# Turning rows and columns in the dense part by transposing DMA transfers, on a TensorE-bound two-layer kernel

## The chip, the cores and the metric

The kernel runs on one core of one Trainium2 chip. The metric is device time in microseconds (us) of one launch. The kernel before was timed in three runs: 1625.38, 1627.13 and 1629.6 us, median 1627.13 us. A profile of one execution shows what each engine did: PE is TensorE (PEld its weight loads), DVE is VectorE, ACT is ScalarE, POOL is GpSimd, SP is the engine whose queue issues most of the transfers.

## The reference

Four stages follow each other on x of 2048 rows by 512 columns, and each adds its result to x: attention A, dense B, attention A, dense B, with the same weights both times.

```python
def _A_ref(x, mem0, Wq, Wk, Wv, Wo, seg_len):          # 32 heads of 128, M = 8, seg_len = 32
    mem = mem0
    for s in range(n_seg):                              # 64 segments, one after the other
        h = jnp.concatenate([mem, xs], axis=1)          # 8 memory rows + 32 rows of x
        q, k, v = (einsum('btd,dhe->bhte', h, W) for W in (Wq, Wk, Wv))
        scores = where(mask, einsum('bhqe,bhke->bhqk', q, k) * scale, -1e9)
        o = einsum('bhqk,bhke->bhqe', _softmax(scores), v)
        o = einsum('bhte,hed->btd', o, Wo)
        mem = o[:, :M, :].copy()                        # the memory of the next segment
        outs.append(o[:, M:, :])
def _B_ref(x, w1, w2):                                  # 512 -> 1376 -> 512
    return einsum('bsf,fd->bsd', maximum(einsum('bsd,df->bsf', x, w1), 0), w2)
x = x + _A_ref(_layernorm(x), A_mem0, ...)
x = x + _B_ref(_layernorm(x), B_w1, B_w2)
x = x + _A_ref(_layernorm(x), A_mem0, ...)
x = x + _B_ref(_layernorm(x), B_w1, B_w2)
```

The memory makes the segments of a layer a strict sequence: segment s+1 cannot start before the output projection of segment s has ended.

## The kernel before, in words

All weights stay in SBUF, in bf16. The kernel runs 68 steps. In step k the first attention layer works on segment k and the second on segment k-4 (`DELTA = 4`), side by side in the same instructions: the columns of `HT` hold 40 rows of the one (8 of memory, 32 of x) and 40 of the other. Steps 0 to 3 have only the first layer, steps 64 to 67 only the second. Within a step the heads come in five units: queries and keys (`queries_keys`), scores and softmax (`scores`), values (`step_values`), attention times values (`attend`), and then the output projection (`project`), whose PSUM bank `st` gives the next memory (evicted to `HT`) and the layer's output columns (evicted to `OX`).

The dense part stands between. After every second step `finish_pair(j)` takes the 64 rows of two segments of the first layer and, side by side, the 64 rows of two segments of the second layer that are done. The steps of it are, with the lines of the profile:

1. `OX` holds the attention's output with columns on the partitions. Four matmuls against the identity turn it into the PSUM bank `y` of the pool `fill` (helper `across`, L665).
2. DVE adds `y` to the rows `x` (tile `xg`, L884).
3. `layernorm` on DVE and POOL (L706, L709, L712, L713) writes the normalised rows to `xr` (L716); four matmuls turn them into another `fill` bank, and ACT or DVE copies that to `xnM` (L919, L921).
4. `dense_layer`: 44 matmul groups on `xnM` with w1, ReLU to `hT` (L765, L767), 11 with w2, and additions (L800, L804) that give the rows of the second layer's input and of the output.
5. For the first layer's half, a second `layernorm`: again four matmuls turn `xr`, and a copy writes `xnB`, from which POOL fills the columns of `HT` (`prep_x`, L941) at the start of the step that needs them.

There are 34 calls of `finish_pair` (30 of them with both halves) and 32 second layernorms. The 16 layernorms of the first layer's groups of 128 rows, marked `halved=True`, use the same function with another layout of the result.

The program's order is not that of the source. Every piece is an `op` of a `Plan` with the engine that it may run on, a cost, what it reads and writes, and a lag to the next engine. `Plan.order()` places them one by one by a priority: for PE work `PERIOD * step + PLACE[...]`, for the rest a due time worked back from it less `AHEAD[...]`; both tables are long lists of numbers. The instructions are then issued in that order on every engine and on every queue. SP's queue carries, per step, two transfers of old values (`V<-vh`, L1018), four of new values (`V<-vw`, L1024), the loads of x, and the stores of the output (L905), each behind the one before it. PSUM has five banks for `work`, one for `st` and two for `fill`.

Of the kernel before, what the change touches and what calls it, by code (L numbers as in the profile page):

```python
# [21 lines left out]
PE, ACT, DVE, POOL, SP, QUEUE = range(6)  # L22
# [4 lines left out]
WHOLE, COL64, EITHER, SOFT = range(4)  # L27
# [3 lines left out]
RULE = (0.0676, 338.0438, 3554579.0286, 1242705613.0663)  # L31
PERIOD = 42.8582
PLACE = {
    ("attend.mmu0.0", 0): 608.991, ("attend.mmu0.0", 1): 157.899, ("attend.mmu0.0", 2): -380.976,
    ("attend.mmu0.0", 3): -849.744, ("attend.mmu0.0", 4): -420.014, ("attend.mmu0.0", 5): 379.888,
    ("attend.mmu0.0", 6): -935.369, ("attend.mmu1.0", 0): 724.653, ("attend.mmu1.0", 1): 735.673,
    ("attend.mmu1.0", 2): 83.429, ("attend.mmu1.0", 3): -335.179, ("attend.mmu1.0", 4): 3.094,
    ("attend.mmu1.0", 5): -935.256, ("attend.mmu1.0", 6): -23.81, ("attend.mmu2.0", 0): -313.198,
    ("attend.mmu2.0", 1): -1055.43, ("attend.mmu2.0", 2): 351.452, ("attend.mmu2.0", 3): -29.526,
    ("attend.mmu2.0", 4): -812.532, ("attend.mmu2.0", 5): 234.539, ("attend.mmu2.0", 6): -65.699,  # L40
    ("attend.mmu3.0", 0): 13.451, ("attend.mmu3.0", 1): 157.484, ("attend.mmu3.0", 2): 133.291,
    ("attend.mmu3.0", 3): -203.514, ("attend.mmu3.0", 4): 192.222, ("attend.mmu3.0", 5): -84.323,
    ("attend.mmu3.0", 6): -139.89, ("attend.mmu4.0", 0): -853.255, ("attend.mmu4.0", 1): -244.026,
    ("attend.mmu4.0", 2): -305.761, ("attend.mmu4.0", 3): -104.638, ("attend.mmu4.0", 4): -89.602,
    ("attend.mmu4.0", 5): -204.344, ("attend.mmu4.0", 6): 50.714, ("dense_layer.mm.0", 1): 822.894,
    ("dense_layer.mm.0", 3): 717.325, ("dense_layer.mm.0", 6): 792.485, ("dense_layer.mm.1", 1): -268.282,
    ("dense_layer.mm.1", 3): 157.778, ("dense_layer.mm.1", 6): -380.794, ("dense_layer.mm.2", 1): 376.492,
    ("dense_layer.mm.2", 3): 130.965, ("dense_layer.mm.2", 6): -212.381, ("dense_layer.mm.3", 1): -70.602,
    ("dense_layer.mm.3", 3): 419.403, ("dense_layer.mm.3", 6): -774.382, ("dense_layer.mm.4", 1): -244.79,
    ("dense_layer.mm.4", 3): 367.889, ("dense_layer.mm.4", 6): -182.649, ("dense_layer.mm.5", 1): 943.633,  # L50
    ("dense_layer.mm.5", 3): -26.387, ("dense_layer.mm.5", 6): 595.003, ("finish_pair.turn.0", 1): -125.119,
    ("finish_pair.turn.0", 3): -175.437, ("finish_pair.turn.0", 6): -732.778, ("g0", 2): -902.623,
    ("g1", 2): -345.827, ("g2", 2): 376.933, ("g3", 2): -860.996, ("g4", 2): 261.098, ("g5", 2): -902.521,
    ("g6", 2): 262.286, ("g7", 2): 447.122, ("late_values.mmv0.0", 0): 7.391, ("late_values.mmv1.0", 0): 723.22,
    ("late_values.mmv2.0", 0): -33.087, ("late_values.mmv3.0", 0): -918.158, ("late_values.mmv4.0", 0): 711.016,
    ("late_values.mmv5.0", 0): -29.506, ("late_values.mmv6.0", 0): -417.119, ("late_values.mmv7.0", 0): -388.807,
    ("layernorm.turn.0", 1): -11.687, ("layernorm.turn.0", 3): 291.45, ("layernorm.turn.0", 6): 74.607,
    ("layernorm.turn.1", 1): 932.83, ("layernorm.turn.1", 3): -23.815, ("layernorm.turnr.0", 0): 130.977,
    ("layernorm.turnr.1", 0): 22.148, ("prepare.turns.0", 2): 138.08, ("project.mm.0", 0): -28.38,
    ("project.mm.0", 1): -813.549, ("project.mm.0", 2): -352.721, ("project.mm.0", 3): 338.425,  # L60
    ("project.mm.0", 4): -85.099, ("project.mm.0", 5): 395.603, ("project.mm.0", 6): 258.346,
    ("project.mm.1", 0): 382.886, ("project.mm.1", 1): 332.847, ("project.mm.1", 2): -815.345,
    ("project.mm.1", 3): 420.621, ("project.mm.1", 4): -904.087, ("project.mm.1", 5): 539.837,
    ("project.mm.1", 6): 66.403, ("project.mm.2", 0): 332.311, ("project.mm.2", 1): -807.177,
    ("project.mm.2", 2): -643.677, ("project.mm.2", 3): 169.374, ("project.mm.2", 4): 38.108,
    ("project.mm.2", 5): 154.46, ("project.mm.2", 6): -123.487, ("project.mm.3", 0): -94.659,
    ("project.mm.3", 1): -2.385, ("project.mm.3", 2): -392.671, ("project.mm.3", 3): 755.857,
    ("project.mm.3", 4): 239.419, ("project.mm.3", 5): 449.254, ("project.mm.3", 6): 237.48,
    ("project.mm.4", 0): -28.331, ("project.mm.4", 1): -89.329, ("project.mm.4", 2): 233.897,
    ("project.mm.4", 3): -897.55, ("project.mm.4", 4): 4.166, ("project.mm.4", 5): -271.575,  # L70
    ("project.mm.4", 6): 68.861, ("queries_keys.mmu0.0", 0): -114.972, ("queries_keys.mmu0.0", 1): -803.223,
    ("queries_keys.mmu0.0", 2): 449.473, ("queries_keys.mmu0.0", 3): -814.936, ("queries_keys.mmu0.0", 4): 64.492,
    ("queries_keys.mmu0.0", 5): -247.66, ("queries_keys.mmu0.0", 6): -321.229, ("queries_keys.mmu0.1", 0): -246.448,
    ("queries_keys.mmu0.1", 1): -83.345, ("queries_keys.mmu0.1", 2): -93.12, ("queries_keys.mmu0.1", 3): -67.094,
    ("queries_keys.mmu0.1", 4): -882.377, ("queries_keys.mmu0.1", 5): -142.63, ("queries_keys.mmu0.1", 6): -836.169,
    ("queries_keys.mmu0.2", 0): -921.465, ("queries_keys.mmu0.2", 1): -331.089, ("queries_keys.mmu0.2", 2): -36.099,
    ("queries_keys.mmu0.2", 3): -153.588, ("queries_keys.mmu0.2", 4): 0.628, ("queries_keys.mmu0.2", 5): -845.834,
    ("queries_keys.mmu0.2", 6): -937.81, ("queries_keys.mmu0.3", 0): -75.904, ("queries_keys.mmu0.3", 1): -26.436,
    ("queries_keys.mmu0.3", 2): -78.722, ("queries_keys.mmu0.3", 3): -83.815, ("queries_keys.mmu0.3", 4): -874.602,
    ("queries_keys.mmu0.3", 5): -285.858, ("queries_keys.mmu0.3", 6): -288.873,  # L80
    ("queries_keys.mmu1.0", 0): -287.689, ("queries_keys.mmu1.0", 1): -807.17, ("queries_keys.mmu1.0", 2): 138.905,
    ("queries_keys.mmu1.0", 3): -775.344, ("queries_keys.mmu1.0", 4): 333.755, ("queries_keys.mmu1.0", 5): -69.094,
    ("queries_keys.mmu1.0", 6): -299.934, ("queries_keys.mmu1.1", 0): -894.335,
    ("queries_keys.mmu1.1", 1): -300.828, ("queries_keys.mmu1.1", 2): -195.096,
    ("queries_keys.mmu1.1", 3): -407.541, ("queries_keys.mmu1.1", 4): -99.416, ("queries_keys.mmu1.1", 5): -928.29,
    ("queries_keys.mmu1.1", 6): -1007.777, ("queries_keys.mmu1.2", 0): -397.855,
    ("queries_keys.mmu1.2", 1): -271.199, ("queries_keys.mmu1.2", 2): -95.574, ("queries_keys.mmu1.2", 3): -424.872,
    ("queries_keys.mmu1.2", 4): -828.244, ("queries_keys.mmu1.2", 5): -84.504, ("queries_keys.mmu1.2", 6): -365.113,
    ("queries_keys.mmu1.3", 0): -267.974, ("queries_keys.mmu1.3", 1): -319.862, ("queries_keys.mmu1.3", 2): 11.67,
    ("queries_keys.mmu1.3", 3): -410.531, ("queries_keys.mmu1.3", 4): 44.01, ("queries_keys.mmu1.3", 5): -391.768,  # L90
    ("queries_keys.mmu1.3", 6): -213.718, ("queries_keys.mmu2.0", 0): -65.556, ("queries_keys.mmu2.0", 1): -240.632,
    ("queries_keys.mmu2.0", 2): 64.693, ("queries_keys.mmu2.0", 3): 448.514, ("queries_keys.mmu2.0", 4): 417.76,
    ("queries_keys.mmu2.0", 5): 347.423, ("queries_keys.mmu2.0", 6): -104.214, ("queries_keys.mmu2.1", 0): -34.178,
    ("queries_keys.mmu2.1", 1): 23.812, ("queries_keys.mmu2.1", 2): -196.254, ("queries_keys.mmu2.1", 3): -337.37,
    ("queries_keys.mmu2.1", 4): 139.933, ("queries_keys.mmu2.1", 5): -92.169, ("queries_keys.mmu2.1", 6): 434.453,
    ("queries_keys.mmu2.2", 0): 129.446, ("queries_keys.mmu2.2", 1): 68.117, ("queries_keys.mmu2.2", 2): -78.718,
    ("queries_keys.mmu2.2", 3): -0.671, ("queries_keys.mmu2.2", 4): 460.034, ("queries_keys.mmu2.2", 5): 252.252,
# [103 lines left out]


def t_dve(n, rate=1):
    return 0.065 + 1.042e-3 * n / rate


PART, MASKED = {ACT: 0.13, DVE: 0.10}, {ACT: 0.11, DVE: 0.065}


def t_pool(n):  # L210
    return 0.06 + 2.2e-3 * n


# [1119 lines left out]
```

## Time and profile before

| | |
|---|---|
| median of 3 runs | 1627.13 us (1625.38 to 1629.6) |
| span of the profiled execution, first to last instruction | 1624.3 us |
| its own time | not listed with the page; the runs' median lies 2.8 us over the span |
| PE busy | 1584.0 us (98%), 43678 matmuls |
| PE weight loads | 1378.5 us (85%) |
| DVE, ACT, POOL busy | 1031.9 us (64%), 1095.1 us (67%), 139.2 us (9%) |
| granted TensorE clock | 0.998 |
| DMA, mean | 39 GB/s over the span |
| two steps in the middle (evictions of `st` to `HT` at 779.41 and 827.52 us) | 48.1 us |

The chain that ended last is followed back from the last instruction to whatever released each one: an engine's share of it is time that the end of the kernel depended on. Matmuls overlap in the pipeline, so the mean of one in the list of groups (200 ns) is a latency; what a matmul costs the stream is the distance to the next, and that is what the chain of a stretch shows.

### The profile page before, as it was taken

What the parts mean: (1) busy time and instruction counts of PE and PEld (TensorE: products, weight loads), DVE (VectorE), ACT (ScalarE), POOL (GpSimd) and SP (SyncE); (2) the same over time, 40 slices, a digit from 0 to 9 for tenths busy, and PEclk for the clock granted to TensorE, in tenths of its full rate; (3) what the DMA queues carried; (4) which work ended last, traced back from release to release, by engine and by line L of the source; (5) the groups of instructions that cost most, each with busy time, mean ns of one, the idle gap of its engine ahead of it and who ended that gap; (6) DMA issues with size and microseconds to landing.
All of it is one profiled execution on the core that took longest, in us unless ns stands there. A gap on an engine that the chain in (4) does not pass through costs nothing.

```text
span 1624.3 us, 95837 instructions
## 1 busy us (share of the span) xinstructions
PE 1584.0 (98%) x43678; PEld 1378.5 (85%) x43746; DVE 1031.9 (64%) x2930; ACT 1095.1 (67%) x2813; POOL 139.2 (9%) x362
## 2 busy tenths in 40 slices
PE   7999999999999999999999999999999999999997
PEld 4688888888888888888888888888888888888886
DVE  4466756666665675676566567566656756665665
ACT  5567767766676776766677676667667766766664
POOL 4210000000000000100000000000000000000000
PEclk9999999999999999999999999999999999999999
DMA  9711001111100110111011011101101000000000
GB/s 372 264 23 33 19 22 29 23 27 34 34 21 21 29 25 25 35 28 26 22 30 25 26 35 28 25 22 26 27 25 28 23 21 19 17 20 19 19 6 6
DMA packets 42885, 63.37 MB, mean 39 GB/s; under 512 B 15400, under 2 KB 28816, under 8 KB 42480
## 3 DMA queue, kind: packets, MB, share of 16 engines
q1 hardware_dynamic: 35984, 35.88, 8.8%
q0 software_dynamic: 5328, 20.32, 3.3%
q8 instruction: 342, 5.60, 1.4%
q10 hardware_dynamic: 1168, 1.06, 0.2%
q14 instruction: 63, 0.52, 0.1%
HBM read 33.50 MB, written 11.93 MB: 28 GB/s over the span
## 4 chain that ended last, share of the span: by engine, by line
PE 94%; DVE 3%; issue 1%; ACT 1%; POOL 0%; DMA 0%; DVEq 0%; POOLq 0%; ACTq 0%
PE work L665 39%; PE st L665 19%; PE fill L998 15%; PE fill L665 12%; PE work L1166 4%; PE work L1082 3%; DVE es L1093 0%; DMA hT<-in_A_x_dram 0%; DVE mx L1097 0%; ACT HT L919 0%; PE fill L789 0%; DVE sm L1107 0%; DVE vw L921 0%; DVE PT L1149 0%; DVE es L1100 0%
## 5 line engine op out<-in xcount | busy, mean ns | idle before, releaser
L665 PE MATMUL work<-HT,Wq_sb 128*128 128x80 bf16 (+2 forms) x10208 | 369.3, 200 | 8.2 <-ACT HT L919 8.1
L665 PE MATMUL work<-HT,Wk_sb 128*128 128x80 bf16 (+2 forms) x10144 | 368.2, 200 | 2.4 <-issue 1.5
L665 PEld LDWEIGHTS <-Wq_sb 128*128 128x128 bf16 (+1 forms) x10208 | 330.4, 103 | 25.8 <-ACT HT L919 11.6
L665 PEld LDWEIGHTS <-Wk_sb 128*128 128x128 bf16 (+1 forms) x10144 | 333.4, 103 | 17.9 <-issue 3.5
L665 PE MATMUL st<-OT,Wo_sb 128*128 128x80 bf16 (+1 forms) x8704 | 339.7, 199 | 3.0 <-ACT OT L919 1.3
L665 PEld LDWEIGHTS <-Wo_sb 128*128 128x128 bf16 x8704 | 319.8, 99 | 11.7 <-issue 4.1
L919 ACT CAST qT<-work 128x320 bf16<-128x320 f32 (+1 forms) x484 | 197.7, 408 | 119.1 <-PE work L665 83.7
L998 PE MATMUL fill<-Wv_sb,HT 128*64 128x512 bf16 x2176 | 272.7, 381 | 0.5 <-POOL HT L938 0.5
L919 ACT CAST kT<-work 128x320 bf16<-128x320 f32 (+1 forms) x539 | 220.1, 409 | 58.5 <-PE work L665 18.7
L1147 ACT ACTIVATE PT<-work,half 128x320 bf16<-128x320 f32 (+2 forms) x448 | 200.6, 467 | 31.5 <-PE work L665 15.0
L919 ACT CAST vw<-fill 128x512 bf16<-128x512 f32 x227 | 132.8, 585 | 105.1 <-PE fill L998 103.0
L919 ACT CAST OT<-work 128x320 bf16<-128x320 f32 (+1 forms) x394 | 151.9, 413 | 76.4 <-PE work L1166 76.3
L1093 DVE TENSOR_TENSOR es<-work,maskb 128x320 f32<-128x320 f32 (+2 forms) x340 | 133.2, 402 | 60.3 <-PE work L1082 48.9
L998 PEld LDWEIGHTS <-HT 128*64 128x64 bf16 x2176 | 106.9, 110 | 70.5 <-issue 0.8
L884 DVE TENSOR_TENSOR xg<-xg,fill 128x512 f32<-128x512 f32 (+1 forms) x34 | 23.4, 688 | 185.9 <-PE fill L665 185.9
L1104 ACT ACTIVATE es<-es 128x320 f32<-128x320 f32 (+2 forms) x340 | 134.8, 406 | 7.4 <-DVE es L1100 3.5
L1100 DVE TENSOR_TENSOR es<-es,mx 128x320 f32<-128x320 f32 (+2 forms) x340 | 133.7, 404 | 2.6
L1097 DVE TENSOR_REDUCE mx<-es 128x8 f32<-128x320 f32 (+2 forms) x340 | 132.1, 399 | 3.6
L1124 DVE TENSOR_TENSOR P<-es,sm 128x320 bf16<-128x320 f32 (+2 forms) x338 | 131.1, 405 | 4.4
L1107 DVE TENSOR_REDUCE sm<-es 128x8 f32<-128x320 f32 (+2 forms) x340 | 130.9, 395 | 1.2 <-ACT es L1104 1.1
L1149 DVE TENSOR_SCALAR PT<-work,half 128x320 bf16<-128x320 f32 (+2 forms) x232 | 103.2, 454 | 26.6 <-PE work L665 24.3
L800 DVE TENSOR_TENSOR xg<-xg,fill 64x512 f32<-64x512 f32 x30 | 20.4, 681 | 140.5 <-PE fill L665 140.5
(98 smaller groups left out, 1801.7 us busy)
## 6 DMA issues: line engine op xcount, KB each, us to landing
V<-vw SPq DMA_DIRECT2D x240, 48.0 KB
V<-vh SPq DMA_DIRECT2D x120, 64.0 KB
Wq_sb<-in_A_Wq_dram POOLq DMA_DIRECT2D x2, 2048.0 KB, 21.0
Wk_sb<-in_A_Wk_dram POOLq DMA_DIRECT2D x2, 2048.0 KB, 25.4
Wo_sb<-in_A_Wo_dram POOLq DMA_DIRECT2D x2, 2048.0 KB, 37.1
vh<-vg SPq DMA_DIRECT2D x32, 128.0 KB
Wv_sb<-in_A_Wv_dram POOLq DMA_DIRECT2D x1, 2048.0 KB, 11.4
vh<-w_sb POOLq DMA_DIRECT2D x4, 512.0 KB, 5.3
```

What stands on the lines that cost most here:

```text
L665: nc.tensor.matmul(out_[u:v, :], lhsT=lhsT[:, u:v], rhs=rhs, start=start, stop=stop, tile_position=(0, u), **more)
L919: nc.scalar.copy(out=out_, in_=in_)
L998: nc.tensor.matmul(vp[64 * b:64 * b + 64, :], lhsT=cols(c4), rhs=Wv_sb[:, c4, n * 512:(n + 1) * 512], start=(c4 == 0), stop=(c4 == NC4 - 1 ...
L1093: nc.vector.tensor_tensor(out=flat(es[:, A]), in0=flat(sp[:, A]), op=ALU.add, in1=maskb[:, a_lo:a_hi, :].unsqueeze(2).to_broadcast([128, n ...
L1097: nc.vector.tensor_reduce(out=mx[:, As], in_=es3(), axis=AX.X, op=ALU.max)
L1100: nc.vector.tensor_tensor(out=es3(), in0=es3(), op=ALU.subtract, in1=mx[:, As].unsqueeze(2).to_broadcast([128, ns * na, L]))
L1104: nc.scalar.activation(out=es[:, A], in_=es[:, A], func=ACTF.Exp, scale=SCALE)
L1107: nc.vector.tensor_reduce(out=sm[:, As], in_=es3(), axis=AX.X, op=ALU.add)
L1124: (nc.gpsimd if eng == POOL else nc.vector).tensor_tensor(out=o, in0=flat(es[:, A]), op=ALU.mult, in1=sm[:, As].rearrange("p (a s) -> p a ...
L1147: nc.scalar.activation(out=o, in_=i, func=ACTF.Copy, scale=half[:, b:b + 1])
L1149: nc.vector.tensor_scalar_mul(out=o, in0=i, scalar1=half[:, b:b + 1])
L1166: nc.tensor.matmul(o[u:u + cols, :, a, :], lhsT=V[:, p, e0 + u:e0 + u + cols], rhs=PT[:, a, 2 * i + h2, :, :], start=True, stop=True, tile ...
```

## The change

In the dense part, the three turns (of `OX`, and of `xr` in both layernorms) are no longer matmuls. Each is one `dma_start_transpose` issued by SP: `OX` goes to a tile `y` in SBUF (of the pool `xr`, which has one buffer), `xr` goes straight to `xnM` or `xnB`. The copies from PSUM to `xnM` and `xnB` fall away, and so does a `fill` bank for each turn. `OX` is turned whole, all 128 rows, also where only one half of them is used; so its two tiles are set to zero by POOL at the start. The 16 `halved` layernorms keep their matmuls. `RULE`, `PLACE`, `AHEAD` and `PAIRED` are other numbers throughout, so that the order of all work is another one.

```diff
-RULE = (0.0676, 338.0438, 3554579.0286, 1242705613.0663)
+RULE = (0.077, 191.201, 3554579.029, 1242705613.066)
 ...
+XBAR = 0.5, 0.2, 2.6
 ...
+        for i, t in enumerate(p_ox.tiles):
+            def zero_ox(t=t):
+                nc.gpsimd.memset(t[:], 0.0)
+
+            plan.op(POOL, 0.4, zero_ox, w=[("oxz", i)])
 ...
     def layernorm(x, rows, xnT, lo=0, n=128, to=None, halved=False):
-        ln, xn, tp = p_ln.buf(), p_xr.buf(), b_fill.buf()
+        ln, xn, tp = p_ln.buf(), p_xr.buf(), b_fill.buf() if halved else None
 ...
-            else:
-                copy_on(eng, xnT[:, :, to:to + n], i.rearrange("p (c t) -> p c t", c=NC4))
+        def turn_far():
+            nc.sync.dma_start_transpose(out=xnT[:, :, to:to + n], in_=xn[R, :])
 ...
         plan.op(DVE, 0.453 + pd, norm, r=[x, ln, *rows], w=[xn])
+        if not halved:
+            plan.op(SP, XBAR[0] + XBAR[1] * NC4 * n / 128, turn_far, r=[xn], w=[xnT], lag=XBAR[2])
+            return xnT
         plan.op(PE, 0.01 + 1.72e-3 * n, turn, r=[xn, "ident"], w=[tp], tile=EITHER, count=4)
 ...
     def finish_pair(j):
-        x, ox, y = x_tiles[j], ox_tiles[j], b_fill.buf()
+        x, ox, y = x_tiles[j], ox_tiles[j], p_xr.buf()
 ...
-        def turn(cols):
-            T = slice(0, 128 if 1 in act else PR)
-            for c4 in range(NC4):
-                across(cols, y[:, c4 * 128:(c4 + 1) * 128], ox[:, c4, T], ident[:])
+        def turn():
+            nc.sync.dma_start_transpose(out=y[:, :].rearrange("t (c d) -> t c d", c=NC4),
+                                        in_=ox[:, :, :].rearrange("p c t -> p (c t)"))
 ...
-        plan.op(PE, 0.23, turn, r=[ox, "ident"], w=[y], tile=EITHER, count=4)
+        plan.op(SP, XBAR[0] + XBAR[1] * NC4, turn, r=[ox], w=[y], lag=XBAR[2])
 ...
-            copy_op(NC4 * SEG * len(aa), rows, r=[wo, ("taken", k)], w=[ox])
+            copy_op(NC4 * SEG * len(aa), rows, r=[wo, ("taken", k), ("oxz", 0), ("oxz", 1)], w=[ox])
```

## The prediction, made before the run

> **What bounds the kernel now.** I began with the page: span, busy shares and the chain that ended last.
>
> ```profile
> span 1624.3 us, 95837 instructions
> PE 1584.0 (98%) x43678; PEld 1378.5 (85%) x43746; DVE 1031.9 (64%) x2930; ACT 1095.1 (67%) x2813; POOL 139.2 (9%) x362
> PE 94%; DVE 3%; issue 1%; ACT 1%; POOL 0%; DMA 0%; DVEq 0%; POOLq 0%; ACTq 0%
> PE work L665 39%; PE st L665 19%; PE fill L998 15%; PE fill L665 12%; PE work L1166 4%; PE work L1082 3%; DVE es L1093 0%; DMA hT<-in_A_x_dram 0%; DVE mx L1097 0%; ACT HT L919 0%; PE fill L789 0%; DVE sm L1107 0%; DVE vw L921 0%; DVE PT L1149 0%; DVE es L1100 0%
> ```
>
> PE carries 94% of the chain; the other engines have a third of the time to spare. The end depends on how much PE has to do, and on little else. The waits of PE's weight loads, for the 60 or so steps with both layers (158 to 1518 us), say how little:
>
> ```profile
> PEld L665 <- ACT HT L919: 11.3, 26, 0.4
> PEld L665 <- DVE P L1124: 6.7, 28, 0.3
> PEld L665 <- issue: 2.8, 9, 0.4
> ```
>
> These three are all: 20.8 us in 1360. PE waits about 0.35 us a step, mostly for the eviction of the new memory to `HT`. So a microsecond taken from PE there is a microsecond off the end, as long as nothing new makes it wait.
>
> What the turns cost PE I read from the chain of two steps in the middle (779.4 to 827.5 us), whose columns are start, length, work:
>
> ```profile
> 783.29 0.22 PE fill L665 x4
> ...
> 787.38 0.22 PE fill L665 x8
> ...
> 826.79 0.12 PE fill L665 x4
> ```
>
> By the timeline of the same stretch these are the turn of `OX` (783.12), of `xr` for `xnM` (787.20, in eight half-width matmuls) and of `xr` for `xnB` (826.63). A pair of steps spends 0.22 + 0.22 + 0.12 = 0.56 us on them. The same timeline shows what lies around them:
>
> ```profile
> 779.52 0.38 ACT L919 CAST OX<-st 128x256 bf16<-128x256 f32 x1
> ...
> 783.55 0.69 DVE L884 TENSOR_TENSOR xg<-xg,fill 128x512 f32<-128x512 f32 x1 [6.13 <-PE fill L665]
> ...
> 786.18 0.55 DVE L716 TENSOR_SCALAR xr<-xg,ln 128x512 bf16<-128x512 f32 x1 [1.00 <-POOL ln L713]
> ...
> 794.10 1.96 PE L665 MATMUL fill<-xnM,w_sb 128*64 128x128 bf16 x64
> ...
> 808.69 0.55 DVE L716 TENSOR_SCALAR xr<-xg,ln 64x512 bf16<-64x512 f32 x1 [0.99 <-POOL ln L713]
> ...
> 827.43 0.52 POOL L941 COPY HT<-xnB 128x128 bf16<-128x128 bf16 x2 [7.59 <-ACT xnB L919]
> ```
>
> `OX` is complete at 779.90, the addition begins at 783.55. `xr` is complete at 786.73 and first used by PE at 794.10, 7.4 us later. The second `xr` is complete at 809.24 and read by POOL at 827.43, 18 us later. There the dense part has time to give away. At the end of the kernel it has none:
>
> ```profile
> 1611.34 0.27 ACT L919 CAST OX<-st 128x128 bf16<-128x128 f32 x1 [0.64 <-PE st L665]
> ...
> 1612.10 0.69 DVE L884 TENSOR_TENSOR xg<-xg,fill 64x512 f32<-64x512 f32 x1 [2.06 <-PE fill L665]
> ...
> 1614.72 0.55 DVE L716 TENSOR_SCALAR xr<-xg,ln 64x512 bf16<-64x512 f32 x1 [0.99 <-POOL ln L713]
> ...
> 1616.16 2.61 PE L665 MATMUL fill<-xnM,w_sb 128*128 128x64 bf16 x44 [0.46 <-ACT xnM L919]
> ...
> 1621.05 0.47 SPq L905 DMA_DIRECT2D out_dram<-ob  x1
> ```
>
> Every row waits for the one above it: the last pair's dense part runs alone.
>
> **What a transfer takes.** No transposing transfer is in this trace, so I bound it by plain ones. The shortest that can be followed on SP's queue is a load of 128 KB in the ramp, issued at 111.70 and awaited by DVE until 113.81, so 2.1 us. The last store (SP, out of SBUF, 64 KB) is issued at 1621.05 and the span ends at 1624.3: 3.2 us at most. Of POOL's issues a 128 KB store took longest, the last of the rows here:
>
> ```profile
> 111.70 0.35 SPq L825 DMA_DIRECT2D xe<-in_A_x_dram  x1
> 113.81 0.69 DVE L706 BATCH_NORM_STATS2 ln<-xe 128x6 f32<-128x512 bf16 x1 [2.38 <-DMA xe<-in_A_x_dram]
> xh<-OX POOLq DMA_DIRECT2D x1, 128.0 KB, 7.1
> ```
>
> So 2.1 to 7.1 us. I take 4.0 us from the source being ready to the result being usable: nearest is the store of 3.2 us, same queue and same source, and a turn moves up to twice its bytes and must be handed from DVE or ACT to SP and back. (The planner books 1.3 us on SP's queue and 2.6 more, the diff's `XBAR`; that is an input of its order and no measurement, and the sum doesn't use it.)
>
> **The change, part by part.**
>
> Removed from PE: 30 full pairs x 0.56 = 16.8 us; pairs 0 and 1 have a half-width `xr` in both layernorms, 0.22 + 0.12 + 0.12 = 0.46 each, 0.9; pair 32 has no second layernorm, 0.34. Sum 18.0 us. The last pair is counted in the tail.
>
> Removed from ACT and DVE: 34 copies to `xnM` (0.69 us on DVE, 0.59 on ACT) and 32 to `xnB` (0.37), some 34 us in all, on engines busy to two thirds. I count nothing: their lateness shows only in PE's 20.8 us, and of that the `HT` wait is a latency, not a load. Two `fill` banks are shared by fewer users; PE waited for no `fill` bank in that list, so nothing again.
>
> Tail: `OX` ready 1611.61 to addition 1612.10 is 0.49 us, becomes 4.0, +3.5. `xr` ready 1615.27 to first matmul 1616.16 is 0.89, becomes 4.0, +3.1. Sum +6.6 us; with 2.1 us it is +2.8, with 7.1 +12.8. [...]
>
> Middle: with 4.0 us, `y` lands at 783.9 (addition 0.4 us later than now), `xnM` at 791.1, before 794.10, and `xnB` at 813.2, before 827.43. At 7.1 us `xnM` would be 3.3 us late and the later 18 us would take that up. Cost 0, unless the order places users too early.
>
> SP's queue: three issues more per pair. Plain issues take 0.36 (`V<-vh`) and 0.72 us (`V<-vw`, median of 120); even 1.5 us each is 4.5 in 48, and the queue mostly waits. What stands behind a turn that waits for `OX` or `xr` are the value transfers, and behind those `attend` on PE. At 783 to 788 and 809 to 813 us the queue was empty, so I count 0; above, it could make `attend` late.
>
> Start: POOL sets two tiles to zero. Its nearest rows are 0.20 us (a memset of a quarter of the tile) and 0.61 (a cast of 64x512), so 0.4 to 1.2 us, on the path only if it stands before a weight load's issue. I take 0, since POOL is free before `OX` is needed at 54 us.
>
> Ramp: pair 0 has its second `xr` at 97.7 and step 4 starts at 111; three turns longer by about 3 us each still fit. Cost 0.
>
> New order: bounded from both sides by PE's waits. A perfect one could win all 20.8 us, one that doubles them would lose 20.8. I take 0, for the same rules and the same limits made it.
>
> Sum: -18.0 + 6.6 = -11.4 us. The profiled span becomes 1612.9; the page lists no time of its own for that execution, and the median of the runs lies 2.8 us over its span, so the forecast is 1615.7 us.
>
> **The rivals.**
>
> *Slow turns.* Each takes 7.1 us, as the slowest 128 KB transfer here. The middle hides it, the tail pays 12.8: -5.2, so 1621.9 us. For it: both are 128 KB and nothing here has shown a transposing one. Against: that row fell in the busiest stretch of DMA (over 260 GB/s).
>
> *The order loses (slower than before).* At the change of step PE waits 0.4 us for `HT`, in 26 of the 57 steps; in the others the last two w2 matmuls (804.84 us, 0.60 us of PE) stand in that gap. The turns were small pieces that could stand anywhere, and the dense work now comes up to 4 us later. If pieces no longer meet the gaps, each of 60 steps loses more. It decides from 11.4 / 60 = 0.19 us a step. If the 0.35 us doubles, it is +20.8: -11.4 + 20.8 = +9.4, so 1636.5 us. For it: every number of the order is new and PE has 1.5% of slack. Against: the rest of PE's work, and so what can fill gaps, is the same.
>
> *Half-way.* The gaps take 0.15 to 0.25 us a step: 1625 to 1630 us, no change.
>
> *Not what it says.* The 16 `halved` layernorms keep PE; 64 of their turns stay, and I've not counted them. So this changes nothing.
>
> **How the numbers follow.** The measurement can tell 0.3% (4.9 us) from no change. Forecast (turns of 2.1 to 5 us, order as good: 1609 to 1619) 0.46; slow turns 0.14, both faster; half-way 0.11; the order loses 0.29. So faster 0.60, same 0.11, slower 0.29. The range goes from 1608 (turns at 2.1 us give 1611.9, an order 4 us better) to 1638, just over the doubled waits: about 5% lie below and 13% above. The forecast's own range is 1609 to 1619.
>
> **What would show it right or wrong.** After the change no `fill<-ident,OX` is left, and `fill<-ident,xr` only for `halved` groups; PE has some 400 to 600 matmuls fewer. The 57 steps between the evictions to `HT` at 158.8 and 1518.5 us take 47.7 us a pair now and would take 47.1. The tail from the last `OX` eviction to the end, 13.0 us now, becomes about 19.6. PE's waits from 158 to 1518 us stay near 21 us. Wrong would be: more than 32 us of waits for `HT`, `P` or `V` there, or waits of PE for `xnM`.

## The result and the profile after

The change took 1620.24 us (median of 4 runs, 1619.77 to 1621.06) against 1627.35 us before (4 runs, 1625.38 to 1629.6): ratio 0.9953, 95% interval 0.9939 to 0.9967. That is 7.1 us faster; 11.4 were forecast (1615.7 us). The profiled execution took 1621.06 us over a span of 1619.3, the slowest of its four.

The page after: span, busy times, then the chain that ended last by engine and by line.

```profile
span 1619.3 us, 94084 instructions
PE 1573.6 (97%) x42673; PEld 1355.0 (84%) x42673; DVE 1050.2 (65%) x2974; ACT 1058.4 (65%) x2672; POOL 160.7 (10%) x395
PE 95%; ACT 2%; DMA 1%; POOL 1%; issue 1%; DVE 1%; POOLq 0%; SPq 0%; DVEq 0%; ACTq 0%
PE work L671 40%; PE st L671 19%; PE fill L1006 16%; PE fill L671 11%; PE work L1174 4%; PE work L1090 3%; ACT OT L927 1%; DMA xr<-OX 0%; ACT HT L927 0%; PE fill L798 0%; DMA xnM<-xr 0%; DMA V<-vw 0%; ACT es L1112 0%; POOL ln L719 0%; ACT qT L927 0%
```

PE is still the bound (95% of the chain) with 1005 matmuls fewer on record. New in the list of lines is `ACT OT L927` with 1%: the eviction before the output projection.

To see where the time went I cut the span at evictions of `st` to `HT`: that of step 5 (158.8 us before, 161.5 after), that of step 62, and that of step 66, the last. "Middle" is the 57 steps that the prediction named.

| us | start to step 5 | middle | step 62 to 66 | last to end | span |
|---|---|---|---|---|---|
| before | 158.8 | 1359.7 | 76.5 | 29.3 | 1624.3 |
| after | 161.5 | 1346.2 | 77.7 | 33.9 | 1619.3 |
| difference | +2.7 | -13.5 | +1.2 | +4.6 | -5.0 |

The medians differ by 7.1 and the two profiled spans by 5.0: each profile is one execution. That of after is 0.8 us over its median. A run's time lies some 1.8 us over its span here (1621.06 and 1619.3), so the profiled one of before is, by estimate, 1.3 us under its median.

**The middle.** By the medians an even step took 25.32 us and takes 24.85; an odd one took 22.13 and takes 22.23. The two turns of the even step (0.44 us of PE) came back in full, the one of the odd step (0.12) did not. The chain shows why. Start, length and work at the end of an odd step, before:

```profile
1205.53 0.43 PE work L1166 x12
1205.96 0.07 PE work L665 x2
1206.03 0.12 PE fill L665 x4
...
1206.18 1.31 PE st L665 x32
```

and at the same place after:

```profile
1151.37 0.16 PE work L1174 x4
...
1151.55 0.43 ACT OT L927
...
1152.03 1.31 PE st L671 x32
```

The four `fill` matmuls (0.12 us) and some others filled the time until `OT` was evicted and the last part of the projection could run. Without them PE stands still for ACT instead. The waits of PE's weight loads from 158 to 1518 us (total, times, longest) say the same:

```profile
PEld L671 <- issue: 17.0, 49, 0.4
PEld L671 <- ACT HT L927: 12.0, 29, 0.4
PEld L671 <- DVE P L1132: 9.6, 26, 0.4
```

38.6 us, and 39.1 with one more row, against 20.8 before. The wait for `HT` stayed; "issue" rose by 14. Of its 17.0 us, 5.1 stand before loads of `Wo_sb`, each of which starts within 0.01 us of a matmul that waited for `OT`. The other 11.9 stand before loads of `Wq_sb`, at one place of the new order, where the chain has no gap. One of them, and the chain there:

```profile
1140.47 1.19 PEld L671 LDWEIGHTS <-Wq_sb 128*128 128x128 bf16 x32 [0.41 <-issue]
...
1139.67 0.86 PE fill L1006 x8
1140.54 3.14 PE work L671 x84
```

So most of the rise costs the stream nothing: the matmuls of the whole stretch waited 4.0 us for `OT` (1.3 before) and 7.9 for `HT`, as before.

**A turn.** All turns of `OX` and all to `xnM`, in the view by tile: ns on SP's queue (min, median, max), first and last start.

```profile
L888 SPq DMA_TRANSPOSE xr<-OX x34: 1190/1237/2829, 78.0 to 1602.1; - x34
L736 SPq DMA_TRANSPOSE xnM<-xr x34: 1171/1215/2024, 86.8 to 1607.8; - x34
```

SP is held for 1.24 us. The tail, by the timeline, shows the whole turn:

```profile
1601.81 0.27 ACT L927 CAST OX<-st 128x128 bf16<-128x128 f32 x1 [1.05 <-PE st L671]
1602.10 1.19 SPq L888 DMA_TRANSPOSE xr<-OX  x1
1604.54 0.69 DVE L892 TENSOR_TENSOR xg<-xg,xr 64x512 f32<-64x512 f32 x1 [3.60 <-DMA xr<-OX]
...
1607.16 0.55 DVE L722 TENSOR_SCALAR xr<-xg,ln 64x512 bf16<-64x512 f32 x1 [0.99 <-POOL ln L719]
1607.77 1.17 SPq L736 DMA_TRANSPOSE xnM<-xr  x1
1610.12 2.61 PE L671 MATMUL fill<-xnM,w_sb 128*128 128x64 bf16 x44 [8.35 <-DMA xnM<-xr]
...
1612.66 2.56 PE L798 MATMUL fill<-w_sb,hT 128*64 128x256 bf16 x22
```

`OX` is ready at 1602.08 and added from 1604.54: 2.46 us (0.49 before). `xr` is ready at 1607.71 and used from 1610.12: 2.41 us (0.89 before). Together +3.5 us. The matmuls with w2 took 2.56 us where they had taken 1.42, +1.1. That is the clock (0.52, before 0.96); the last but two figures of a row are the granted clock, the DMA share follows. After, w1 and w2:

```profile
1610.10:1612.60 2.50, 2.48 (x44) 2.48 (x43) 0.00 (x0) 0.77 (x2) 0.00 (x0) 0.50 0.02 7
1612.60:1615.30 2.70, 2.62 (x24) 1.78 (x22) 0.26 (x2) 0.28 (x1) 0.00 (x0) 0.52 0.00 0
```

and w2 before:

```profile
1618.70:1620.20 1.50, 1.42 (x23) 1.15 (x22) 0.25 (x2) 0.28 (x1) 0.00 (x0) 0.96 0.00 0
```

w1 ran at half clock in both (0.50; before from 1616.10 to 1618.70 us). In the trace's record of the clock the low stretch lasts 3.4 us before (1615.39 to 1618.81) and 10.2 after (1604.96 to 1615.20). PE had stood idle for 3.3 us before the turn of `xr` at 1615.33, and with the change it does so for 8.4 us before w1. What sets the length of the low stretch is not shown.

### The profile page after: what moved, and what is told of

Its sections match the earlier page's. It is cut to its first block, busy times and chain, and to the rows that moved or that the text cites. A ratio compares the mean times of both kernels' runs of the same rounds, so it can differ in the third digit from the quotient of the medians.

```text
span 1619.3 us, 94084 instructions
## 1 busy us (share of the span) xinstructions
PE 1573.6 (97%) x42673; PEld 1355.0 (84%) x42673; DVE 1050.2 (65%) x2974; ACT 1058.4 (65%) x2672; POOL 160.7 (10%) x395
## 3 DMA queue, kind: packets, MB, share of 16 engines
q10 hardware_dynamic: 1168, 1.06, 0.2%
## 4 chain that ended last, share of the span: by engine, by line
PE 95%; ACT 2%; DMA 1%; POOL 1%; issue 1%; DVE 1%; POOLq 0%; SPq 0%; DVEq 0%; ACTq 0%
PE work L671 40%; PE st L671 19%; PE fill L1006 16%; PE fill L671 11%; PE work L1174 4%; PE work L1090 3%; ACT OT L927 1%; DMA xr<-OX 0%; ACT HT L927 0%; PE fill L798 0%; DMA xnM<-xr 0%; DMA V<-vw 0%; ACT es L1112 0%; POOL ln L719 0%; ACT qT L927 0%
## 5 line engine op out<-in xcount | busy, mean ns | idle before, releaser
L671 PE MATMUL work<-HT,Wk_sb 128*128 128x80 bf16 (+2 forms) x9184 | 357.3, 199 | 11.5 <-ACT HT L927 9.3
L671 PE MATMUL work<-HT,Wq_sb 128*128 128x80 bf16 (+2 forms) x10624 | 357.6, 200 | 0.0
L1006 PE MATMUL fill<-Wv_sb,HT 128*64 128x512 bf16 x2176 | 281.8, 383 | 0.9 <-POOL HT L946 0.5
L927 ACT CAST kT<-work 128x320 bf16<-128x320 f32 (+1 forms) x517 | 211.8, 410 | 107.5 <-PE work L671 66.3
L927 ACT CAST qT<-work 128x320 bf16<-128x320 f32 (+1 forms) x505 | 207.7, 412 | 73.7 <-PE work L671 25.7
L927 ACT CAST OT<-work 128x320 bf16<-128x320 f32 (+1 forms) x351 | 132.6, 414 | 129.2 <-PE work L1174 128.6
L1155 ACT ACTIVATE PT<-work,half 128x320 bf16<-128x320 f32 (+1 forms) x406 | 181.8, 477 | 8.7 <-DVE PT L1157 4.0
L927 ACT CAST vw<-fill 128x512 bf16<-128x512 f32 x228 | 133.9, 587 | 76.3 <-PE fill L1006 73.4
L1157 DVE TENSOR_SCALAR PT<-work,half 128x160 bf16<-128x160 f32 (+2 forms) x274 | 116.2, 445 | 31.4 <-PE work L671 29.7
L892 DVE TENSOR_TENSOR xg<-xg,xr 128x512 f32<-128x512 f32 (+1 forms) x34 | 23.5, 692 | 161.1 <-DMA xr<-OX 160.9
L1090 PEld LDWEIGHTS <-qT 128*40 128x40 bf16 x4096 | 87.4, 98 | 34.6 <-ACT qT L927 0.3
```

The source lines that it names most:

```text
L671: nc.tensor.matmul(out_[u:v, :], lhsT=lhsT[:, u:v], rhs=rhs, start=start, stop=stop, tile_position=(0, u), **more)
L927: nc.scalar.copy(out=out_, in_=in_)
L1006: nc.tensor.matmul(vp[64 * b:64 * b + 64, :], lhsT=cols(c4), rhs=Wv_sb[:, c4, n * 512:(n + 1) * 512], start=(c4 == 0), stop=(c4 == NC4 - 1 ...
L1090: nc.tensor.matmul(v[64 * g2:64 * g2 + L, a, i, b, :], lhsT=qT[:, hi, a * L:(a + 1) * L], rhs=kT[:, hi, a * L:(a + 1) * L], start=True, st ...
L1155: nc.scalar.activation(out=o, in_=i, func=ACTF.Copy, scale=half[:, b:b + 1])
L1157: nc.vector.tensor_scalar_mul(out=o, in0=i, scalar1=half[:, b:b + 1])
```

## The experiments

Each is timed against the kernel before on the chip that it ran on (medians there 1629.26, 1629.21 and 1627.99 us), so kernels of different groups are compared by their ratios, and parts of the span by the cuts above. The change's own ratio is 0.9953.

**1. No turns at all, in the order of before** (`no_turns`). What is PE's work on turns worth?

```diff
-            for c4 in range(NC4):
+            for c4 in range(NC4 if halved else 0):
 ...
-            T = slice(0, 128 if 1 in act else PR)
-            for c4 in range(NC4):
-                across(cols, y[:, c4 * 128:(c4 + 1) * 128], ox[:, c4, T], ident[:])
+            pass
```

> The kernel before in its own order, unchanged but for the matmuls of the dense part's turns: they are left out, so the additions and copies read what the bank held. It is the change with turns that cost nothing at all. Theory A (PE's stream): every turn was PE time on the path, so 34 of OX, 34 and 32 of xr give 18.3 us: 1609 us. Theory B (fillers): a turn also stood where PE would have waited anyway, as the xnB turn before the last output projection of an odd step; there it gives back nothing, so some 30 x 0.12 us less: 1612 to 1613 us, with odd steps near 22.1 us as before. Theory C (the new order is the weak part of the change): like A, and the middle (eviction to HT of step 5 to that of step 62) falls by 16.5 us or more.

Measured: 1606.89 us, ratio 0.9866 (0.9851 to 0.9881). That is under the totals of all three theories, since leaving out the matmuls leaves out waits as well: in the last pair the addition begins at 1596.19 us and `OX` is evicted only at 1597.46, so the tail (24.0 us from the last `HT`, 29.3 before) can't be compared. The middle can, as a lower bound. It is 1345.8 us, 13.9 shorter than before; an even step is 24.87 us (-0.45), an odd one 22.13, as before: theory B. At the end of an odd step the place of the four matmuls is taken by the wait:

```profile
1148.68 0.43 ACT OT L917
...
1149.15 1.31 PE st L665 x32
```

So 13.9 us is all that the middle could give in that order, and the change has 13.5 of it. The second layernorm's turn was filler, and its 30 x 0.12 = 3.6 us were counted for nothing.

**2. The turns alone, in the order of before** (`turns_alone`): the transfers issued where the matmuls, or the norm, stood.

```diff
+            if not halved:
+                nc.sync.dma_start_transpose(out=xnT[:, :, to:to + n], in_=xn[R, :])
 ...
-            for c4 in range(NC4):
-                across(cols, y[:, c4 * 128:(c4 + 1) * 128], ox[:, c4, T], ident[:])
+            nc.sync.dma_start_transpose(out=y_t[:, :].rearrange("t (c d) -> t c d", c=NC4),
+                                        in_=ox[:, :, :].rearrange("p c t -> p (c t)"))
```

> The kernel before in its own order of operations, with the dense part's turns as transposing transfers: OX is issued where the PE turn stood, xr right behind its normalisation, the copies from PSUM left out, one OX tile set to zero in step 0. No order planned anew. If the turns alone make the gain (A), it is the run without turns plus the tail's 4.6 us, about 1614 to 1616 us, and faster than the change. If new order and change belong together because a transfer lands 2.4 us after it is ready where PE took 0.5 to 0.9, DVE's queue is held at the addition behind y and PE is late by up to 2 us a pair: over 1640 us. If SP's queue is the trouble (value transfers behind the turns), PE waits for V appear.

Measured: 1625.88 us, ratio 0.9981 (0.9972 to 0.9990), between the totals that were expected. Middle 1346.7 us, half a microsecond from the change's. It loses elsewhere: 81.5 us from step 62 to 66 (76.5 before, 77.7 with the change), and 3.5 us in step 4, whose chain has the turn of `OX`:

```profile
112.02 4.82 DMA y_t<-OX
```

In that step the clock is low as well, from 120.26 to 123.67 us: eight `fill` matmuls with `Wv_sb` take 1.71 us on the chain there, where eight took 0.86 in the piece of the change's chain above. So the new order is worth nothing in the middle. It is worth 3.8 us from step 62 to 66 and 4.1 in step 4 (24.5 us with the change), where the old one has the users of a turn too close behind it; the rest of the start is quicker in the old order, and eats that up (161.1 us to the eviction of step 5, 161.5 with the change).

**3. Every turn twice** (`turns_twice`), the first into a spare tile: is there room for a later turn?

```diff
+            nc.sync.dma_start_transpose(out=spare_t[:, :, 0:n], in_=xn[R, :])
             nc.sync.dma_start_transpose(out=xnT[:, :, to:to + n], in_=xn[R, :])
 ...
+            nc.sync.dma_start_transpose(out=spare_t[:, :, :], in_=ox[:, :, :].rearrange("p c t -> p (c t)"))
             nc.sync.dma_start_transpose(out=y[:, :].rearrange("t (c d) -> t c d", c=NC4), ...
```

> The changed kernel, same order, with each transposing transfer made twice, the first time into a spare tile. The turn then lands 1.2 us (one more issue) to 2.4 us (a whole turn) later, and SP and DMA carry 100 of them more. If the dense part's slack in the middle hides a turn, the middle stays at 1346 us and only the tail grows, by 2.4 to 4.8 us: 1622.6 to 1625 us. If transfers cost something in the middle (value transfers late, instruction fetch or SBUF disturbed), the 66 pairs of issues there show it: 0.3 us each would be 20 us, over 1640 us.

Measured: 1652.09 us, ratio 1.0141 (1.0127 to 1.0155), some 31 us over the change (0.0188 of 1629); 20.6 of them are in the middle. The chain by engine:

```profile
PE 80%; DVE 8%; DMA 7%; ACT 2%; issue 2%; POOL 1%; SPq 1%; DVEq 0%; POOLq 0%
```

Where the room ends shows on DVE. With the change, one pair in the timeline:

```profile
921.07 0.69 DVE L892 TENSOR_TENSOR xg<-xg,xr 128x512 f32<-128x512 f32 x1 [4.96 <-DMA xr<-OX]
...
924.42 0.49 DVE L1101 TENSOR_TENSOR es<-work,maskb 128x320 f32<-128x320 f32 x1 [1.71 <-PE work L1090]
```

DVE adds `y`, has 1.71 us to spare, and starts the softmax when PE's scores arrive. The same pair with every turn twice:

```profile
938.75 0.69 DVE L895 TENSOR_TENSOR xg<-xg,xr 128x512 f32<-128x512 f32 x1 [8.37 <-DMA xr<-OX]
...
940.30 0.47 DVE L1104 TENSOR_TENSOR es<-work,maskb 128x320 f32<-128x320 f32 x1
```

No idle time stands before the softmax now: its scores were there at 938.57, and DVE came to them at 940.30. The addition that waited in DVE's queue held the softmax behind it for 1.7 us. `OX` had been ready for 5.9 us; with the change it was 2.5, so 1.7 us of lateness are free and the rest is paid by PE.

**4 and 5. Only the turn of `OX` twice, only those of `xr` twice** (`ox_twice`, `xr_twice`): the lines of experiment 3, one at a time.

> The changed kernel, same order, with only the transfer of OX made twice (first into a spare tile), so that y lands some 3.4 us later, as in the run with all turns twice. Theory D (DVE's queue): the addition of y stands ahead of the next softmax in DVE's queue; behind the addition DVE has only about 1.7 us of waiting left, so what y is later than that PE waits for P. Then this run has most of the 32 us that all turns twice cost: 1638 to 1650 us, with even steps over 25 us and PE waiting for P. Theory E (traffic: transfers as such disturb PE or the value transfers): a third of them is doubled, so a third of the loss, about 1630 us.

> The changed kernel, same order, with only the 66 transfers of xr made twice. Theory D: no DVE work stands behind them, xnM has 3 us to spare and xnB 14, so the middle stays within 3 us of the change and the tail grows by 1.2 to 2.4 us: 1621.5 to 1626 us. Theory E (traffic): two thirds of the loss of all turns twice, about 1641 us.

Measured: 1636.39 us, ratio 1.0050 (1.0036 to 1.0064), and 1636.85 us, 1.0047 (1.0033 to 1.0060); middles 1360.4 and 1358.9 us, 14.3 and 12.7 over the change. `OX` loses by DVE's queue as above: its time lies just under theory D's range and above E's 1630, and the waits of matmuls for `P` that D named are there (5.9 us from 158 to 1508 us, none with the change). That `xr` would cost next to nothing was wrong: the new order needs `xnM` about 5.0 us after the turn's issue, not after the 7.4 us that stood between `xr` and its use before, and PE waits for it:

```profile
PE fill L672 <- DMA xnM<-xr: 9.4, 11, 1.5
```

A piece of its chain has the turn itself:

```profile
842.14 4.35 DMA xnM<-xr
...
846.53 0.49 PE fill L672 x11
```

4.35 us for a turn that took 2.4 in the tail. That transposing traffic holds up the value transfers instead doesn't show: matmuls waited 0.6 us for `V` here and 0.4 with the change. Two turns in a row seemed to run one after the other; experiments 6 and 7 were made for that.

**6 and 7. The same bytes without a turn, once and twice** (`plain`, `plain_twice`): plain transfers between the same tiles.

```diff
-            nc.sync.dma_start_transpose(out=xnT[:, :, to:to + n], in_=xn[R, :])
+            nc.sync.dma_start(out=xnT[:, :, to:to + n], in_=xn[:, 0:NC4 * n].rearrange("t (c d) -> t c d", c=NC4))
 ...
+            nc.sync.dma_start(out=y[:, :], in_=ox[:, :, :].rearrange("p c t -> p (c t)"))
```

> The changed kernel, same order, with each transposing transfer replaced by a plain one of the same bytes between the same tiles (nothing is turned). If a transposing transfer is no slower than a plain one (F), y is ready 2.4 to 2.5 us after the issue as in the change, and the time is within 2 us of it: 0.9945 to 0.9965 of before. If transposing adds to the transfer (G), the addition starts under 2.2 us after the issue, the tail is about 0.6 us shorter or more, and SP is held for 0.4 to 0.7 us instead of 1.2. By G the value transfers behind the turns may gain as well: up to 4 us less than the change.

> The same with each of the plain transfers made twice, the first into a spare tile. Theory H (the loss of 32 us with all turns twice is that of two transposing transfers in a row, the second of which lands some 4 us after its issue): plain ones overlap, the second lands about 0.7 us (one issue) later than a single one, within the 1.7 to 2.6 us that the order leaves, so under 5 us over the run with plain ones once. Theory E (100 further transfers as such cost it, through SP's queue and the DMA engines): 30 us more, as with transposing ones.

Measured: 1618.22 us, ratio 0.9936 (0.9922 to 0.9949), and 1620.83 us, 0.9949 (0.9936 to 0.9962). A plain transfer holds SP 0.53 us (1.24) and is used 2.07 us after its issue (2.50), so a turn does cost more than a plain transfer (theory G). Doubling costs 2.6 us instead of 31: the second is used 2.13 us after its issue. So far theory H had its numbers, and E, by which any further transfers cost it, is out. The landings of the turns refute H as well. In `ox_twice` I took all 29 second turns of `OX` in the middle, and beside them the 16 KB packets of the queue that the page calls `instruction` (there are 342 in the kernel before with its 95837 instructions, 334 with the change's 94084; that they carry the program's own code is my reading of these counts and not shown). One pair, by the DMA view of 883.4 to 885.6 us, queue and packets, MB, share of 16 engines, and the next pair, 931.1 to 933.3:

```profile
q1 hardware_dynamic: 1075, 0.26, 60.0%
q8 instruction: 1, 0.02, 2.5%
...
q1 hardware_dynamic: 1073, 0.26, 59.4%
```

and what the timeline has of the two:

```profile
883.43 1.26 SPq L890 DMA_TRANSPOSE xr<-OX  x1
...
887.50 0.69 DVE L894 TENSOR_TENSOR xg<-xg,xr 128x512 f32<-128x512 f32 x1 [7.85 <-DMA xr<-OX]
...
931.13 1.26 SPq L890 DMA_TRANSPOSE xr<-OX  x1
...
933.63 0.69 DVE L894 TENSOR_TENSOR xg<-xg,xr 128x512 f32<-128x512 f32 x1 [6.30 <-DMA xr<-OX]
```

Both turns are second ones, 1.28 us behind the first. With a packet of instructions among its own the turn is used after 4.07 us, without one after 2.50. In the first, 15 of its 16 completions came 2.37 to 2.50 us after the issue and the 16th at 4.04; the packet had started 1.99 us after the issue. The 29 turns fall into three groups by that start: at 1.99 to 2.16 us one completion is late (7 turns), earlier, up to 1.84, all 16 are (16 turns), and from 2.28 us on, or with no packet, none is (6). Over the middle, sorted by whether such a packet started between 0.45 us before the issue and 2.2 us after it (1.75 for plain ones), issue to addition:

| turn of `OX` | with a packet: count, median us | without: count, median us |
|---|---|---|
| after | 9, 4.04 | 20, 2.50 |
| `ox_twice`, second | 23, 4.03 | 6, 2.50 |
| `turns_twice`, second | 23, 4.01 | 6, 2.53 |
| `xnB_pe` (below) | 29, 3.86 | 0 |
| `plain` | 5, 2.40 | 24, 2.07 |
| `plain_twice`, second | 8, 3.51 | 21, 2.13 |

Without a packet a second turn takes as long as a single one, so they don't run one after the other. What the second loses is 1.28 us of SP's queue, which moves it into the time, some 2 to 4 us after `OX`, at which most pairs have a packet (23 of 29). This is sorted from traces and no experiment of its own: a kernel that moves the packets alone wasn't run, and why an early packet holds up the whole turn isn't shown.

**8. The second layernorm's turn on PE again** (`xnB_pe`), at a priority behind all other work.

```diff
+    ("layernorm.turn.0", 1): 100000, ("layernorm.turn.0", 3): 100000, ("layernorm.turn.0", 6): 100000,
 ...
-            xnT_tiles[(1, j)] = layernorm(x2, [("x", j + D2, 1)], p_xn[1].buf(), PR, PR, 0)
+            xnT_tiles[(1, j)] = layernorm(x2, [("x", j + D2, 1)], p_xn[1].buf(), PR, PR, 0, near=True)
```

> The change, but the second layernorm's turn stays on PE, with its PSUM bank and copy, at the lowest priority: PE takes it where nothing else can start. The order is planned anew by the same numbers from there on. If that turn costs PE nothing because it stands in the wait for the last evictions of OT in an odd step (theory B), odd steps stay at 22.1 to 22.2 us and the time within 2 us of the change. If it is PE time on the path (theory A), odd steps take 0.12 us more: 3.6 us over the change.

Measured: 1620.43 us, ratio 0.9945 (0.9932 to 0.9957), the change's time. PE has 156 matmuls more on record, and the odd step is 22.13 us as before. Here the turn costs PE nothing. Its middle (1345.5 us) shows the room from another side: all 29 turns of `OX` met a packet, `y` was added 3.96 us after `OX` was ready, and no time was lost.

**9. The last pair by PE** (`tail_pe`).

```diff
+        near = j == NP + D2 - 1
 ...
+        if near:
+            plan.op(PE, 0.23, turn_near, r=[ox, "ident"], w=[y], tile=EITHER, count=4)
+        else:
+            plan.op(SP, XBAR[0] + XBAR[1] * NC4, turn, r=[ox], w=[y], lag=XBAR[2])
```

> The changed kernel, but the last finish_pair turns OX and xr by matmuls and a PSUM copy as before; all else in the same order up to there. Theory 1 (latency alone): the two turns of the tail cost 1.97 and 1.5 us more than on PE, so 3.5 us less than the change, 1616.7 us. Theory 2 (latency and clock): PE idles 8.4 us in that tail and its 22 matmuls with w2 then ran at half the granted clock (2.56 us where 1.42 before), so 4.6 us less, 1615.6 us. If the tail is not the place of the loss: no change.

Measured: 1615.18 us, ratio 0.9916 (0.9902 to 0.9929): faster than both kernels. From the last `HT` to the end it is 30.2 us, 3.7 less than with the change. That is theory 1's 3.5, although the total is nearer to theory 2's: the start is 2.2 us shorter (159.3 us), where this edit changes nothing, and the w2 matmuls still take 2.25 us (the low clock lasts 6.8 us here).

**10. PE kept busy in the tail** (`tail_busy`), to see whether the clock then stays up.

```diff
+            for _ in range(140 if j == NP + D2 - 1 else 0):
+                nc.tensor.matmul(b_work.tiles[0][:, 0:128], lhsT=ident[:], rhs=ident[:], start=True, stop=True)
```

> The changed kernel, same order, with 140 matmuls of the identity by itself into an unused bank after the last projection, so that PE is busy while the last two turns and the layernorm run. If PE's clock is lowered by idling in the tail, as the granted 0.50 from 1606 to 1615 us says, the 44 matmuls with w1 (2.61 us) and the 22 with w2 (2.56 us) run at full clock, in about 1.4 us each: 2.3 us less than the change. If the transfers are the whole loss there: no difference.

Measured: 1621.89 us, ratio 0.9954 (0.9941 to 0.9968), no difference. In the timeline:

```profile
1601.25 7.98 PE L891 MATMUL work<-ident 128*128 128x128 bf16 x140
...
1601.73 2.14 SPq L888 DMA_TRANSPOSE xr<-OX  x1
...
1605.00 0.69 DVE L894 TENSOR_TENSOR xg<-xg,xr 64x512 f32<-64x512 f32 x1 [4.44 <-DMA xr<-OX]
...
1608.23 1.17 SPq L736 DMA_TRANSPOSE xnM<-xr  x1
...
1611.68 2.01 PE L671 MATMUL fill<-xnM,w_sb 128*128 128x64 bf16 x44 [2.46 <-DMA xnM<-xr]
...
1613.62 2.53 PE L798 MATMUL fill<-w_sb,hT 128*64 128x256 bf16 x22
```

w1 gained 0.6 us (2.01 for 2.61), its clock being full until 1612.6 (0.99 from 1610.0). But the turns were used 3.3 and 3.5 us after their issue (2.4 with the change). The DMA view has one packet of instructions in each, and none in the change's, and all 16 completions of both were late. The kernel has 335 packets in all, the change 334; whether the 140 matmuls put them there is not shown. Then the clock was low for 3.4 us after all (0.50 from 1612.6 us on), and w2 took 2.53 us.

## Why the prediction was right or wrong

- **The bound and the direction: right.** A chain that is 94% PE gives back what PE no longer does; the middle got 13.5 of the 13.9 us that experiment 1 found there.
- **The PE term: too large.** The step that failed is "30 full pairs x 0.56". It took every matmul on the chain for time. The 0.12 us of `xnB` stood in front of a wait for `OT`, 3.6 us of the 18.0. And the 2.0 us or so counted for the pairs outside the middle didn't show: the start is 2.7 us longer and steps 62 to 66 are 1.2 longer. Start times of kernels with the change's order scatter from 159.3 to 162.6 us, so I can't say which part of the 2.7 is the change; the two memsets of `OX` weren't tried apart. Of the 2.7, 2.4 lie before the first eviction to `HT` (54.5 us, 56.9 after); without turns, in the order of before and with no memsets, it came at 56.1. The PE term and not the turns is the larger error: -18.0 counted, -9.6 found outside the tail.
- **The turn: right in kind, too long.** 4.0 us was taken, 2.4 to 2.5 measured, near the lower bound of 2.1: in the tail 2.46 for the four blocks of 128x128 of `OX`, 2.41 for `xr`.
- **The tail: +6.6 counted, +4.6 found.** 3.5 are turns, 1.1 the clock. That the clock could be low for 10.2 us, where it had been for 3.4, was not thought of, and it is luck that it made up for a third of what the turns were taken too long. The tail's 2.0 us also hide part of the PE term's 8.4.
- **SP's queue and start at 0.** SP is held 1.24 us a turn, within the 1.5 allowed, and PE's matmuls waited for `V` once in the middle, 0.4 us. Right there; the start is told above.
- **"The middle hides it", in the rival of slow turns: wrong.** That rival put turns of 7.1 us at 1621.9 us. The room was read from `xnM` and `xnB` in the old order, and DVE's queue was left out. There is 1.7 us of it behind `y` (experiment 3) and 2.6 behind `xnM` (needed 5.0 us after the issue, there after 2.4). Doubled turns, with `y` added 5.4 us after `OX`, cost some 31 us: turns as slow as that rival's would, by that, have ended on the slower side.
- **The order: 0 was right for the middle** (experiments 1, 2 and the change are within 1 us there). The rival of a losing order didn't come about. But the new order is needed at the ends: without it only 0.9981 is left.
- **The signs.** No `fill<-ident,OX` is left and PE has 1005 matmuls fewer on record (400 to 600 were named): 540 are turns, and 544 come from the new order, which does the same products with `Wq_sb` and `Wk_sb` in fewer half-width matmuls. A pair of steps takes 47.24 us on average over the middle where 47.1 was named, by the missing 0.12. From the last `OX` eviction's start to the end it is 17.5 us, not 19.6. PE's waits were to stay near 21 us and rose to 39.1; those for `HT`, `P` and `V`, whose limit was 32, are 21.6, and none is for `xnM`. The sum of the waits was a bad sign, since it goes by weight loads, which can be late without holding up a matmul.

## What to carry to other kernels

Before counting removed matmuls as time, look at what stands next on the chain after each of them: a piece in front of a wait is filler and was worth nothing here (0.12 us an odd step, 3.6 in all). When a step becomes a transfer, its room is the idle time in front of the next urgent work in the queue of the engine that waits for it, not the time until its own result is used: 1.7 us behind `y` in DVE's queue here. Keep the quick path where nothing runs beside it: the last pair by PE alone took 3.7 us off the end.

## What the hardware showed that was not expected

- Turns that met a packet of instructions were used later. Such a packet took 1.06 us (median; 334 of 16 KB in 1619 us), and a turn of `OX` with one was used 4.0 us after its issue, one without 2.5 (medians of the change, `ox_twice` and `turns_twice`). In `ox_twice` one of the turn's 16 completions was late where the packet started 1.99 to 2.16 us after the issue (7 turns), and all 16 where it started earlier (16 turns); in `xnB_pe` all 16 were late in 24 of 29 turns.
- A transposing transfer of 128x512 bf16 held SP's queue for 1.24 us, a plain one of the same bytes for 0.53. The turn's result was used 2.50 us after the issue, the plain one's after 2.07.
- The low clock at the end lasted 3.4, 6.8 or 10.2 us (before, `tail_pe`, after), and w2 took 1.42, 2.25 or 2.56 us with it. In `turns_twice`, `ox_twice` and `xnB_pe` the mean granted clock of the profiled execution was 0.994, 0.995 and 0.995; it was 0.998 before and 0.997 with the change.
